# A gated linear recurrence with a two-expert router: another order for the first chunk, and fills moved out of the start

## The chip, the cores and the metric

The kernel runs on one core of a Trainium2 chip. The metric is the device time in microseconds of one execution. A core has a matrix engine (TensorE, PE in the profile; its weight loads are listed apart as PEld), a vector engine (VectorE, DVE), a scalar engine (ScalarE, ACT), a general engine (GpSimd, POOL) and a queue that issues most transfers (SyncE, SP). Each engine works through its own instructions in order and waits at an instruction until what it needs is there.

## What is computed

First a recurrence over 768 steps for 4 batches and 8 heads of width 48. Its rows, 3072 of them with 384 numbers each, are the input of a layer of 8 experts of which each row uses the two with the highest noisy logits:

```python
state = alpha[:, :, t, :, None] * state + einsum('bhd,bhe->bhde', k[:, :, t], v[:, :, t])
y[:, :, t] = einsum('bhd,bhde->bhe', q[:, :, t], state)
...
noisy_logits = x @ w_gate + log1p(exp(x @ w_noise)) * noise
top2 = argpartition(-noisy_logits, 2, axis=1)[:, :2]      # weights: softmax over the two
out[mask] += top2_w[mask, k, None] * (maximum(x[mask] @ w1[e], 0.0) @ w2[e])
```

## The kernel before

The recurrence is worked in 24 chunks (`NT`) of 128 steps, six to a batch. For each chunk there are four loads of 192 KB (alpha, k, q, v). The steps of one chunk are these functions, and the hand-written order of their calls is the order of the instructions on every engine (the block under `manual_schedule`, from L1032 of the profile's numbering):

- `alphas(n)`: TensorE turns the alphas (four transposes, L315), ScalarE copies them from PSUM into `a_all` (L323), VectorE scans them into running products `P_all` (L326), takes a reciprocal (L331) and scans backwards into `over` (L332). There is one `a_all`, one `P_all` and one `over`, so a chunk's scan waits for the readers of the last one's.
- `keys(n)`: four transposes, a copy to `k_P` on ScalarE (L341), a sum on ScalarE that checks the range of the alphas (L344), and on GpSimd the product with `over` (L345).
- `queries(n)`: four transposes, the product with `P_all` on VectorE to `q_P` (L354), and a copy of the last column to `P_end` on GpSimd (L355).
- `scores(n)`: 16 products on TensorE (L365). `masked(n)`: two masked copies on VectorE (L370) into one of two `MT` tiles. `turn_k(n)`: four transposes (L377) and a copy to `k_end` on ScalarE (L379).
- `state(n)`: 16 products (L392), an addition on VectorE (L394), a product on GpSimd (L395).
- `output(n)`: 32 products (L242, L246), a copy on ScalarE (L249). `turn_y(n)`: four products with `to_rows` (L261), which bring the rows and the router's logits, and copies (L264, L267). `put_y(n)` stores the rows.

Iteration n of the main loop holds the later steps of chunk n and the earlier ones of chunks n + 1 and n + 2, loads chunk n + 4, and has the router's steps between. Iteration 0 begins when the steps in front of it are done: all of chunk 0 up to its masked scores, and alphas, keys and queries of chunk 1.

Input tiles rotate over three buffers for each of alpha, k and q. They are 64 columns wide for each head, with 48 of data; the rest is filled once by GpSimd (L281). `transposed` takes its four results from a pool `tp` of two PSUM banks; `output` takes its bank from a pool `y` of one.

Before the loop each engine fills constants: GpSimd the identity, masks, expert numbers and regions (L99 and L100, one column at a time), counters (L105 to L114), the matrix `to_rows` (L171 to L174), the input pads (L281), the states (L300) and the row buffers of the experts, `x_in` and `prev` (L814); VectorE `a_all`, `least` and `MT` (L285 to L296) and a cast of the token numbers from integers (L107), the last before the first scan. `to_rows` is first read in iteration 1, after `place_router` (L188) has put the router's weights into it; `x_in` and `prev` are first written by the gathers from iteration 21 on.

From iteration 23 the tiles of the experts (L871, L883) run beside the last chunks and then alone, up to the end.

Of the kernel before, what the change touches and what calls it, by code (L numbers as in the profile page):

```python
# [9 lines left out]
F32 = mybir.dt.float32  # L10
U32 = mybir.dt.uint32
I32 = mybir.dt.int32
# [6 lines left out]
def kernel(  # L19
# [30 lines left out]
    nc = tc.nc  # L50
    B, H, S, D = q.shape
    N, DM = out.shape
    E, _, F = moe_w1.shape
    C = 128
    DP = 64
# [39 lines left out]
    expert_idv = const.tile([C, EV], F32, name="expert_idv")  # L95
    expert_ids = expert_idv[:, 0:E]
    region = const.tile([C, EV], F32, name="region")
    for e in range(EV):
        nc.gpsimd.memset(expert_idv[:, e:e + 1], float(e))  # L99
        nc.gpsimd.memset(region[:, e:e + 1], float(e * RMAX))  # L100
    before = const.tile([C, C], F32, name="before")
    nc.gpsimd.affine_select(out=before, in_=ones, pattern=[[1, C]], compare_op=ALU.is_gt, fill=0.0, base=0,
                            channel_multiplier=-1)
    token = const.tile([C, NT], I32, name="token")
    nc.gpsimd.iota(token, pattern=[[C, NT]], base=0, channel_multiplier=1)  # L105
    token_f = const.tile([C, NT], F32, name="token_f")
    nc.vector.tensor_copy(out=token_f, in_=token)  # L107
    tile_no = const.tile([C, NTILE], F32, name="tile_no")
    nc.gpsimd.iota(tile_no, pattern=[[1, NTILE]], base=0, channel_multiplier=0, allow_small_or_imprecise_dtypes=True)
    full_at = const.tile([C, RMAX // C], F32, name="full_at")  # L110
# [14 lines left out]
    def clear_table(on):  # L125
        entries.clear()
        nothing = on.tile([C, KO * F], F32, tag="w1", name="nothing")[:, 0:TROWS // C * 4]
        nc.vector.memset(nothing, 0.0)
        nc.vector.memset(nothing.rearrange("p (r w) -> p r w", w=4)[:, :, 0:1], float(NONE))
        cleared = nc.scalar.dma_start(out=table.bitcast(F32).rearrange("(p r) w -> p (r w)", p=C), in_=nothing)  # L130
        entries.append(cleared.ins)
# [21 lines left out]
    def rows(src, n):  # L153
        b, c = divmod(n, NCH)
        return src[b, :, ds(c * C, C), :].rearrange("h p d -> p h d")

    def load_chunk(n, ins):
        for x, src in (("a", alpha), ("k", k), ("q", q)):
            nc.sync.dma_start(out=ins[x][n % NIN][:, :, 0:D], in_=rows(src, n))

    def load_values(n, vp):
        vt = vp.tile([C, H, D], F32, name="vt")
# [5 lines left out]

    to_rows = const.tile([C, NP, 2 * D + 2 * E], F32, name="to_rows")

    nc.gpsimd.memset(to_rows, 0.0)  # L171
    for i in range(2):
        for odd in range(2):
            nc.gpsimd.tensor_copy(  # L174
                out=to_rows.rearrange("p (j o) c -> p j o c", o=2)[:, :, odd, ds(2 * E * odd + D * i, D)],
                in_=ident[:, None, ds(DP * i, D)].to_broadcast([C, NP // 2, D]))

    def load_router(on):
        w_r = on["one"].tile([C, NP, 2, E], F32, name="w_r")
        nc.gpsimd.memset(w_r, 0.0)  # L180
        for w, src in enumerate((moe_w_gate, moe_w_noise)):
            for i, part in enumerate(src.rearrange("(j i d) e -> i d j e", i=2, d=D)):
                nc.sync.dma_start(out=w_r[ds(DP * i, D), :, w, :], in_=part)
        return w_r, load_noise(on)
# [89 lines left out]
    def fast_gla(on):  # L274
# [6 lines left out]
                nc.gpsimd.memset(t[:, :, D:DP], 1.0 if x == "a" else 0.0)  # L281

        CB = C + 1
        a_all = one.tile([C, NP * CB + 1], F32, name="a_all")
        nc.vector.memset(a_all, 0.0)  # L285
        a_s = a_all[:, 0:NP * CB].rearrange("p (j t) -> p j t", t=CB)
        least = one.tile([C, NP, C + 1], F32, name="least")
        nc.vector.memset(least, RANGE)
        nc.vector.memset(least[:, :, 0:1], 1.0)
# [10 lines left out]
            nc.gpsimd.memset(t, 0.0)  # L300
        chunks = {}

        def load(n):
            if n < NT:
                chunks[n] = {}
                load_chunk(n, ins)

        def load_v(n):
            if n < NT:
# [8 lines left out]
        def alphas(n):  # L318
            if n >= NT:
                return  # L320
            c = chunks[n]
            a_t = transposed(ins["a"][n % NIN])
            nc.scalar.copy(a_s[:, :, 1:C + 1], a_t)  # L323
            P_all = one.tile([C, NP * CB + 1], F32, name="P_all")
            P = c["P"] = P_all[:, 0:NP * CB].rearrange("p (j t) -> p j t", t=CB)
            nc.vector.tensor_tensor_scan(P_all[:, 0:NP * CB], a_all[:, 0:NP * CB],  # L326
                                         least.rearrange("p j t -> p (j t)"), 0.0, op0=ALU.mult, op1=ALU.max)


            over = c["over"] = one.tile([C, NP, CB], F32, name="over")  # L330
            nc.vector.reciprocal(out=P_all[:, CB::CB], in_=P_all[:, C::CB])  # L331
            nc.vector.tensor_tensor_scan(over.rearrange("p j t -> p (j t)")[:, :0:-1], a_all[:, :1:-1],  # L332
                                         P_all[:, :1:-1], 0.0, op0=ALU.mult, op1=ALU.max)
# [359 lines left out]
    def put_some(n):  # L693
        for place, entry in to_put[:n]:
            put_entries(place, entry)
        del to_put[:n]
# [111 lines left out]
    def experts(on):  # L808
# [1 line left out]
        NB = 3  # L810
        x_in = [one.tile([C, DM], F32, name=f"x_in{i}") for i in range(NB)]
        prev = [one.tile([C, DM], F32, name=f"prev{i}") for i in range(2)]
        for t in x_in + prev:
            nc.gpsimd.memset(t, 0.0)  # L814
        WHY = "computed from the counts, in range by construction"
        tabs, w1s, xts, os_, wheres = {}, {}, {}, {}, {}
        puts, gets, waiting = [], [], []
# [93 lines left out]
                tc.declare_no_dep(put.ins, earlier, reason="different rows, or one that this tile has read")  # L911
            puts.append(put.ins)

        return load_tab, load_w1, gather_x, turn_x, layer1, layer2, get_first, scale, combine, waiting

    def tile_steps(i, do, units, last=False):
        load_tab, load_w1, gather_x, turn_x, layer1, layer2, get_first, scale, combine, waiting = do

        def first():
            if i + 2 < units[1]:
                gather_x(i + 2, units[0])
            layer1(i, 0)

        def second():
            layer1(i, 1)

        def third():
            if i + 1 < units[1]:  # L930
                turn_x(i + 1)
            if i + 2 < units[1]:
                load_w1(i + 2)
            if i - 1 in waiting:
                waiting.remove(i - 1)
                combine(i - 1)
            if last:
                get_first(i)
            layer2(i, 0)

        def fourth():
            layer2(i, 1)
            if last:
                combine(i)
            else:
                scale(i)
                get_first(i)
                waiting.append(i)

        return [first, second, third, fourth]  # L950

    def pools(es, name):
        on = {"one": pool(name + "one", 1, es), "two": pool(name + "two", 2, es), "three": pool(name + "three", 3, es),
              "tab": pool(name + "tab", 6, es)}
        for x, bufs in (("h", 2), ("o", 1), ("tp", 2), ("sc", 1), ("y", 1)):
            on[x] = pool(name + "ps_" + x, bufs, es, space=PS)
        return on


    def last_tiles(i, do):  # L960
        if i == NTILE:
            return
        number = nc.values_load(tiles_i[0:1, 0:1], min_val=0, max_val=NTILE,
                                skip_runtime_bounds_check_because="a count of tiles")
        with tc.If(number > i):
            do[0](i, NU)
            do[1](i)
            do[2](i, NU)
            do[3](i)
            for step in tile_steps(i, do, (NU, i + 1), True):  # L970
                step()
            last_tiles(i + 1, do)


    def again_by_levels():
        with ExitStack() as es:
            on = pool("g_clear", 1, es)
            clear_table(on)
        with ExitStack() as es:
            general_gla(es)  # L980
        with ExitStack() as es:
            do = experts(pools(es, "g_"))
            for i in range(4):
                do[0](i, NU)
            for i in range(2):
                do[1](i)
                do[2](i, NU)
            do[3](0)
            for i in range(NTILE):
                do[0](i + 4, NU)  # L990
                for step in tile_steps(i, do, (NU, NTILE), i >= NTILE - 1):
                    step()


    with ExitStack() as es:
# [33 lines left out]
        beside = [[] for n in range(TILES_AT)] + [list(range(i, min(i + 2, ALWAYS))) for i in range(0, ALWAYS, 2)]  # L1029
        assert 2 * (NT + 5 - TILES_AT) + 4 <= FULL  # L1030

        with tc.manual_schedule():  # L1032
            load(0)
            load_v(0)
            load(1)
            alphas(0)
            keys(0)
            queries(0)
            load(2)
            scores(0)  # L1040
            masked(0)
            turn_k(0)
            alphas(1)
            keys(1)
            queries(1)
            load_v(1)
            load(3)
            for n, tiles in enumerate(beside):
# [3 lines left out]
                          lambda: more_w2(w2_beside.get(n, 0)), lambda: turn_k(n + 1), lambda: output(n),  # L1052
                          lambda: turn_y(n - 1)]
                chunk = [lambda piece=piece, place=place: (piece(), route(n, place)) for place, piece in enumerate(pieces)]
                last = [lambda: put_some(3)]
                if n > NT:
                    chunk.insert(5, lambda: put_some(3))
# [2 lines left out]
                if n == 1:  # L1060
                    chunk.insert(6, lambda: place_router(held.pop(0)))
                    last.append(lambda: clear_table(on["two"]))
                if n == 2:
                    chunk.insert(1, lambda: turn_noise(held.pop(), on))
                if n == NT + 1:
# [63 lines left out]
```

## Time and profile before

| what | value |
|---|---|
| median of 3 runs | 762.68 us (760.94 to 763.94) |
| the profiled execution: time | 764.23 us |
| its span, first to last instruction | 762.5 us |
| granted TensorE clock, mean | 0.989 |
| TensorE busy | 732.9 us (96%) |
| VectorE, ScalarE, GpSimd busy | 240.9, 184.9, 289.8 us |
| chain that ended last: TensorE's share | 69% |
| its largest lines | L871 28%, L883 26% |

The chain's share by engine says where the program's end comes from: more than half of it is the two layers of the experts. The start is a small part of it, and is read from the timeline.

### The profile page before, as it was taken

To read this page: it belongs to the slowest core of one execution; us is meant where nothing else is said; L and a number is where in the kernel's file an instruction comes from. 1 tells how busy PE (TensorE), PEld (TensorE's weight loads), DVE (VectorE), ACT (ScalarE), POOL (GpSimd) and SP (SyncE) were. 2 spreads that over 40 slices of the span, in tenths; PEclk is the share of its full clock that TensorE was granted. 3 is DMA by queue.
4 is the path that set the end of the run, shared out by engine and by line. 5 is a ranking of instruction groups with operands and counts; after the bars stand their busy time and mean duration, and the time that the engine had idled before them with its cause. 6 is when DMAs were issued, how large, how long until landed. Compare 5 with 4: busy or idle time off the path is not lost.

```text
span 762.5 us, 14806 instructions
## 1 busy us (share of the span) xinstructions
PE 732.9 (96%) x5479; PEld 595.0 (78%) x5479; DVE 240.9 (32%) x778; ACT 184.9 (24%) x385; POOL 289.8 (38%) x409
## 2 busy tenths in 40 slices
PE   5999999997999999999999999999999999999996
PEld 3888877876878778877877887788778877888774
DVE  6777867895011223221111101111111111111111
ACT  3455554452112121111111111111111111111110
POOL 4322474765132544453223332333233323333222
PEclk9999999998899999999999999999999999999999
DMA  9999877878789955654565445544565466556631
GB/s 152 156 150 150 140 124 134 138 162 295 243 214 362 320 179 165 196 206 151 200 225 196 145 176 205 185 164 165 204 213 167 174 209 217 181 170 217 225 131 34
DMA packets 149027, 141.80 MB, mean 186 GB/s; under 512 B 111721, under 2 KB 123607, under 8 KB 148948
## 3 DMA queue, kind: packets, MB, share of 16 engines
q1 hardware_dynamic: 136580, 116.58, 54.3%
q0 software_dynamic: 12224, 23.78, 10.3%
q8 instruction: 47, 0.77, 0.4%
q10 hardware_dynamic: 144, 0.41, 0.2%
q14 instruction: 32, 0.26, 0.1%
HBM read 131.95 MB, written 15.25 MB: 193 GB/s over the span
## 4 chain that ended last, share of the span: by engine, by line
PE 69%; issue 11%; DVE 9%; POOL 4%; DMA 4%; ACT 1%; another core or an unknown queue 0%; POOLq 0%; DVEq 0%; ACTq 0%
PE h_ps L871 28%; PE o_ps L883 26%; PE tp L315 3%; DMA x_in<-x_rows,where 2%; PE h_ps L261 2%; PE y L246 2%; PE x_ps L860 2%; PE y L242 2%; PE sc L365 2%; DMA prev<-out_dram,where 2%; DVE over L332 2%; DVE P_all L326 1%; POOL out_dram L908 1%; DVE MT L370 1%; POOL table L134 1%
## 5 line engine op out<-in xcount | busy, mean ns | idle before, releaser
L871 PEld LDWEIGHTS h_ps<-xt,w 128*128 128x128 f32 x2448 | 284.0, 194 | 14.7 <-DVE again L428 1.6
L871 PE MATMUL h_ps<-xt,w 128*128 128x128 f32 x2448 | 285.0, 277 | 2.1 <-DVE again L428 1.4
L883 PE MATMUL o_ps<-w,h 128*128 x816 | 272.2, 487 | 0.2 <-ACT h L873 0.2
L883 PEld LDWEIGHTS o_ps<-w,h 128*128 128x128 f32 x816 | 151.0, 190 | 95.4 <-issue 0.7
L862 DVE COPY xt<-x_ps 128x384 f32<-128x384 f32 x51 | 28.4, 557 | 390.3 <-PE x_ps L860 308.8
L890 POOL DMA_INDIRECT prev<-out_dram,where x51 | 52.9, 1036 | 234.1 <-DMA out_dram<-prev,where 225.4
L873 ACT ACTIVATE h<-h_ps 128x512 f32<-128x512 f32 x102 | 60.9, 597 | 229.5 <-PE h_ps L871 207.3
L908 POOL DMA_INDIRECT out_dram<-prev,where x51 | 52.3, 1025 | 105.7 <-DVE tab L845 76.4
L899 ACT ACTIVATE o<-o_ps,tab 128x384 f32<-128x384 f32 x49 | 28.4, 580 | 235.3 <-PE o_ps L883 230.7
L851 POOL DMA_INDIRECT x_in<-x_rows,where x51 | 52.7, 1034 | 25.0 <-issue 20.6
L134 POOL DMA_INDIRECT table<-entry,place_u x48 | 49.9, 1039 | 14.0 <-issue 12.8
L315 PE MATMUL tp<-ident,w 128*128 128x128 f32 x288 | 44.5, 291 | 9.0 <-DMA w<-in_alpha_dram 4.2
L345 POOL TENSOR_TENSOR k_P<-k_P,over 128x512 f32<-128x512 f32 x24 | 28.4, 1184 | 58.6 <-DVE over L332 52.2
L904 DVE SCALAR_TENSOR_TENSOR prev<-prev,tab,o 128x384 f32<-128x384 f32 x49 | 30.0, 611 | 59.9 <-DMA prev<-out_dram,where 59.9
L315 PEld LDWEIGHTS tp<-ident,w 128*128 128x128 f32 x288 | 32.3, 146 | 14.7 <-POOL w L281 4.7
L326 DVE TENSOR_TENSOR_SCAN P_all<-a_all,least 128x516 f32<-128x516 f32 x24 | 30.8, 1284 | 16.7 <-ACT a_all L323 8.7
L365 PE MATMUL sc<-q_P,k_P 48*128 48x128 f32 x384 | 30.8, 292 | 3.6 <-POOL k_P L345 3.3
L370 DVE COPY_PREDICATED MT<-upto,sc 128x512 f32<-128x512 uint32 x48 | 32.1, 722 | 2.9 <-PE sc L365 2.9
L365 PEld LDWEIGHTS sc<-q_P,k_P 48*128 48x128 f32 x384 | 25.6, 193 | 8.3 <-issue 4.1
L332 DVE TENSOR_TENSOR_SCAN over<-a_all,P_all 128x515 f32<-128x515 f32 x24 | 30.2, 1259 | 0.8
L860 PE MATMUL x_ps<-ident,x_in 128*128 128x128 f32 x153 | 25.2, 274 | 4.0 <-DMA x_in<-x_rows,where 3.8
L261 PE MATMUL h_ps<-to_rows,yT 128*128 128x112 f32 x192 | 28.5, 293 | 0.5 <-POOL to_rows L188 0.5
(153 smaller groups left out, 483.1 us busy)
## 6 DMA issues: line engine op xcount, KB each, us to landing
w<-in_moe_w_dram SPq DMA_DIRECT2D x51, 1536.0 KB
w<-in_moe_w_dram SPq DMA_DIRECT2D x32, 384.0 KB
w<-in_alpha_dram SPq DMA_DIRECT2D x24, 192.0 KB
w<-in_k_dram SPq DMA_DIRECT2D x24, 192.0 KB
w<-in_q_dram SPq DMA_DIRECT2D x24, 192.0 KB
vt<-in_v_dram SPq DMA_DIRECT2D x24, 192.0 KB
x_rows<-y_sb SPq DMA_DIRECT2D x24, 192.0 KB
x_in<-x_rows,where POOLq DMA_INDIRECT x51
```

The source lines that it names most:

```text
L134: put = nc.gpsimd.indirect_dma_start(out=table, out_offset=bass.IndirectOffsetOnAxis(ap=place, axis=0), in_=entry, in_offset=None, bounds_ ...
L261: nc.tensor.matmul(bank[:, at:at + W], yT[:, j, :], to_rows[:, j, :], start=j == 0, stop=j % 2 == 1, skip_group_check=True)
L315: nc.tensor.transpose(tp[:, j, :], src[:, 2 * j:2 * j + 2, :], ident)
L332: nc.vector.tensor_tensor_scan(over.rearrange("p j t -> p (j t)")[:, :0:-1], a_all[:, :1:-1], P_all[:, :1:-1], 0.0, op0=ALU.mult, op1=ALU.max)
L365: nc.tensor.matmul(c["sc"][i][:, j, :], c["k"][r, j, :], c["q"][r, j, :], start=True, stop=True)
L851: nc.gpsimd.indirect_dma_start(out=x_in[i % NB], out_offset=None, in_=x_rows[0:units * UT, :], in_offset=bass.IndirectOffsetOnAxis(ap=wher ...
L860: nc.tensor.transpose(x_ps[:, a, :], x_in[i % NB][:, ds(a * C, C)], ident)
L871: nc.tensor.matmul(h_ps[:, fo, :], w1[:, a, ds((part * FO // 2 + fo) * C, C)], xt[:, a, :], start=a == 0, stop=a == KO - 1)
L873: nc.scalar.activation(os_[i]["h"][part], h_ps, AF.Relu)
L883: take_w2(i, nc.tensor.matmul(o["ps"], o["h"][part][:, f, :], w2[:, ds(o["e"], 1), fo, :].rearrange("p o d -> p (o d)"), start=fo == 0, st ...
L890: get = nc.gpsimd.indirect_dma_start(out=prev[i % 2].bitcast(U32), out_offset=None, in_=out.bitcast(U32), in_offset=bass.IndirectOffsetOnA ...
L908: put = nc.gpsimd.indirect_dma_start(out=out, out_offset=bass.IndirectOffsetOnAxis(ap=where[:, 0:1], axis=0), in_=rows, in_offset=None, bo ...
```

## The change

It has five parts.

1. Constants. Expert numbers and regions are written by one counter instruction each. The token numbers are counted straight into a float tile; the integer tile and VectorE's cast are gone.
2. Fills. `to_rows` is filled in `load_router`, which is called in iteration 0; `x_in` and `prev` are filled at the end of iteration 2 (`clear_rows`).
3. Two `a_all` tiles take turns, and both are filled at the start.
4. Order. The alphas of chunk 1 are loaded right after chunk 0's alpha, k and q, ahead of v. `alphas(1)` stands in front of `scores(0)`, and `keys(1)` behind it. In iteration 0, `scores(1)` stands ahead of `keys(2)`.
5. Twelve products of `ones` with itself on TensorE whose result is not read: six ahead of `alphas(0)`, one each behind it and behind `keys(0)`, four ahead of `scores(0)`.

```diff
-    for e in range(EV):
-        nc.gpsimd.memset(expert_idv[:, e:e + 1], float(e))
-        nc.gpsimd.memset(region[:, e:e + 1], float(e * RMAX))
+    nc.gpsimd.iota(expert_idv, pattern=[[1, EV]], base=0, channel_multiplier=0, allow_small_or_imprecise_dtypes=True)
+    nc.gpsimd.iota(region, pattern=[[RMAX, EV]], base=0, channel_multiplier=0, allow_small_or_imprecise_dtypes=True)
...
-    token = const.tile([C, NT], I32, name="token")
-    nc.gpsimd.iota(token, pattern=[[C, NT]], base=0, channel_multiplier=1)
     token_f = const.tile([C, NT], F32, name="token_f")
-    nc.vector.tensor_copy(out=token_f, in_=token)
+    nc.gpsimd.iota(token_f, pattern=[[C, NT]], base=0, channel_multiplier=1, allow_small_or_imprecise_dtypes=True)
...
-    nc.gpsimd.memset(to_rows, 0.0)
-    for i in range(2):
...
+    def place_ident():
+        nc.gpsimd.memset(to_rows, 0.0)
+        for i in range(2):
...
     def load_router(on):
         w_r = on["one"].tile([C, NP, 2, E], F32, name="w_r")
         nc.gpsimd.memset(w_r, 0.0)
+        place_ident()
...
-        a_all = one.tile([C, NP * CB + 1], F32, name="a_all")
-        nc.vector.memset(a_all, 0.0)
-        a_s = a_all[:, 0:NP * CB].rearrange("p (j t) -> p j t", t=CB)
+        a_alls = [one.tile([C, NP * CB + 1], F32, name=f"a_all{i}") for i in range(2)]
+        for t in a_alls:
+            nc.vector.memset(t, 0.0)
...
-        for t in x_in + prev:
-            nc.gpsimd.memset(t, 0.0)
+
+        def clear_rows():
+            for t in x_in + prev:
+                nc.gpsimd.memset(t, 0.0)
+
...
+        def warm(times):
+            for _ in range(times):
+                nc.tensor.matmul(on["y"].tile([C, NP, C], F32, tag="y", name="y")[:, 0, :], ones, ones, start=True, stop=True)
+
         with tc.manual_schedule():
             load(0)
+            load(1, "a")
             load_v(0)
-            load(1)
+            load(1, "kq")
+            warm(6)
             alphas(0)
+            warm(1)
             keys(0)
+            warm(1)
             queries(0)
+            alphas(1)
             load(2)
+            warm(4)
             scores(0)
+            keys(1)
             masked(0)
             turn_k(0)
-            alphas(1)
-            keys(1)
             queries(1)
             load_v(1)
             load(3)
...
+                if n == 0:
+                    chunk[2], chunk[3] = chunk[3], chunk[2]
...
+                if n == 2:
+                    last.append(do[-1])
```

More of the change, by code (lines that the diff above doesn't have):

```diff
@@ L155, in rows, with load_chunk @@
         return src[b, :, ds(c * C, C), :].rearrange("h p d -> p h d")
-    def load_chunk(n, ins):
+    def load_chunk(n, ins, parts="akq"):
         for x, src in (("a", alpha), ("k", k), ("q", q)):
-            nc.sync.dma_start(out=ins[x][n % NIN][:, :, 0:D], in_=rows(src, n))
+            if x in parts:
+                nc.sync.dma_start(out=ins[x][n % NIN][:, :, 0:D], in_=rows(src, n))
     def load_values(n, vp):
@@ L169 @@
     to_rows = const.tile([C, NP, 2 * D + 2 * E], F32, name="to_rows")
-    nc.gpsimd.memset(to_rows, 0.0)
-    for i in range(2):
[L173 to L176, printed above, removed]
+    def place_ident():
+        nc.gpsimd.memset(to_rows, 0.0)
+        for i in range(2):
+            for odd in range(2):
+                nc.gpsimd.tensor_copy(
+                    out=to_rows.rearrange("p (j o) c -> p j o c", o=2)[:, :, odd, ds(2 * E * odd + D * i, D)],
+                    in_=ident[:, None, ds(DP * i, D)].to_broadcast([C, NP // 2, D]))
     def load_router(on):
@@ L301, in fast_gla, with load @@
         chunks = {}
-        def load(n):
+        def load(n, parts="akq"):
             if n < NT:
-                chunks[n] = {}
-                load_chunk(n, ins)
+                chunks.setdefault(n, {})
+                load_chunk(n, ins, parts)
         def load_v(n):
@@ L322, in alphas @@
             a_t = transposed(ins["a"][n % NIN])
-            nc.scalar.copy(a_s[:, :, 1:C + 1], a_t)
+            a_all = a_alls[n % 2]
+            nc.scalar.copy(a_all[:, 0:NP * CB].rearrange("p (j t) -> p j t", t=CB)[:, :, 1:C + 1], a_t)
             P_all = one.tile([C, NP * CB + 1], F32, name="P_all")
@@ L912, in combine @@
             puts.append(put.ins)
-        return load_tab, load_w1, gather_x, turn_x, layer1, layer2, get_first, scale, combine, waiting
+        return load_tab, load_w1, gather_x, turn_x, layer1, layer2, get_first, scale, combine, waiting, clear_rows
     def tile_steps(i, do, units, last=False):
-        load_tab, load_w1, gather_x, turn_x, layer1, layer2, get_first, scale, combine, waiting = do
+        load_tab, load_w1, gather_x, turn_x, layer1, layer2, get_first, scale, combine, waiting, clear_rows = do
         def first():
@@ L960, in last_tiles @@
     def last_tiles(i, do):
+        if i == ALWAYS:
+            do[-1]()
         if i == NTILE:
@@ L982, in again_by_levels @@
             do = experts(pools(es, "g_"))
+            do[-1]()
             for i in range(4):
```

## The prediction

> **What bounds the kernel now.** I read the page's slices first, then a table of engine times by stretch, then the first 31 us instruction by instruction, then the DMA queue's own waits.
>
> ```profile
> PE   5999999997999999999999999999999999999996
> ```
>
> From the second slice (19 us each) to the last TensorE is busy. What shortens the program is TensorE work taken out, or TensorE idle time; slice one is half idle. By stretch (length, then busy time and count of PE, PEld, DVE, ACT, POOL, then granted clock, DMA share, GB/s):
>
> ```profile
> 0.00:4.00 4.00, 0.00 (x0) 0.00 (x0) 2.51 (x6) 1.28 (x1) 3.22 (x36) 1.00 0.52 93
> 4.00:8.00 4.00, 3.26 (x12) 2.15 (x12) 4.00 (x3) 1.78 (x4) 4.00 (x18) 1.00 1.48 175
> 8.00:16.00 8.00, 4.90 (x31) 4.22 (x32) 3.71 (x8) 1.52 (x3) 1.38 (x3) 1.00 1.53 166
> 16.00:24.00 8.00, 6.35 (x90) 5.22 (x90) 7.21 (x10) 3.20 (x8) 2.78 (x5) 1.00 1.35 147
> 24.00:32.00 8.00, 7.46 (x107) 6.37 (x104) 6.44 (x11) 4.04 (x10) 2.52 (x7) 1.00 0.89 142
> 32.00:45.00 13.00, 12.98 (x160) 11.06 (x160) 8.76 (x13) 6.37 (x16) 3.10 (x5) 1.00 0.85 166
> ```
>
> The PE column idles 10.0 of the first 32 us and 0.02 of the next 13. So the change is worth what it shifts the point, near 32 us, from which TensorE runs without gaps; later stages move along. Why TensorE idles there, in the timeline (start, us, engine, line):
>
> ```profile
> 4.20 3.46 PE L315 MATMUL tp<-ident,w 128*128 128x128 f32 x12 [4.20 <-DMA w<-in_alpha_dram]
> 4.23 3.88 DVE L107 CAST token_f<-token 128x24 f32<-128x24 int32 x1
> 5.94 2.18 DVE L326 TENSOR_TENSOR_SCAN P_all<-a_all,least 128x516 f32<-128x516 f32 x1
> ...
> 9.78 1.17 POOL L345 TENSOR_TENSOR k_P<-k_P,over 128x512 f32<-128x512 f32 x1 [1.70 <-DVE over L332]
> 10.89 0.19 POOL L355 COPY P_end<-P_all 128x4 f32<-128x4 f32 x1
> 11.00 2.08 PE L365 MATMUL sc<-q_P,k_P 48*128 48x128 f32 x16 [3.34 <-POOL k_P L345]
> ...
> 15.74 1.23 DVE L326 TENSOR_TENSOR_SCAN P_all<-a_all,least 128x516 f32<-128x516 f32 x1 [1.29 <-issue]
> ...
> 19.83 1.16 PE L365 MATMUL sc<-q_P,k_P 48*128 48x128 f32 x16
> ...
> 19.94 1.52 DVE L326 TENSOR_TENSOR_SCAN P_all<-a_all,least 128x516 f32<-128x516 f32 x1 [0.65 <-POOL P_end L355]
> ```
>
> A cast of 24 numbers takes 3.88 us, and chunk 0's scan, normally 1.23, ends with it at 8.12. Chunk 1's scan starts only at 15.74, because its transposes stand behind the scores in TensorE's queue. And the first 16 score products take 2.08 where the next 16 take 1.16.
>
> **The cast.** It runs exactly as long as GpSimd does (4.23 to 8.11; GpSimd is busy to 8.08), so GpSimd's fills may be the reason. The change takes both away, so one answer serves: scan 0 ends at 5.94 + 1.23 = 7.17, 0.95 earlier. The rest of that chain keeps its distances: `over` 0 ends at 8.67, `k_P` 0 at 10.0, `P_end` 0 at 10.13, and the scores can start at 10.05. The second `a_all` fill (0.49 and a gap) puts VectorE's fills at 4.86, 1.1 before the scan: nothing.
>
> **Chunk 1's scan.** It needs `P_end` 0 done (one `P_all` buffer) and its transposes, which now stand ahead of the scores. So it starts at 10.17, not 15.74. VectorE then goes on: `over` 1 11.65 to 12.88, the two masked copies of chunk 0 (1.33) to 14.2, `q_P` 1 (0.67) to 14.86. Before, `q_P` 1 ended at 19.03.
>
> **TensorE beside it.** Scores of chunk 0 10.05 to 11.2 at the later speed (1.16), keys 1 (0.6) to 11.8, turned k (0.5) to 12.3. ScalarE copies `k_P` 1 (0.58), does its sum (0.62 and 0.19), copies `k_end` (0.58): 13.75. State products (0.6) to 14.4, alphas 2 (0.6) to 15.0. So the scores of chunk 1 start at 15.05 instead of 19.83: 4.8 earlier. But before, the keys of chunk 2 already lay in front of them; now they lie behind. From 15.05, scores 1.09, keys 0.59, queries 0.59, turned k 0.44, outputs 1.02 + 1.01, state 0.60, alphas 3 0.54 sum to 5.88: 20.93, against 24.97 (24.43 + 0.54). **4.05 us earlier**, and TensorE is from there on its own bound: the first product with `to_rows` comes at 26.2 instead of 30.21.
>
> **The products nobody reads.** Twelve. Six run in front of the first transposes, from about 1.35 (`ones` is there at 1.27). The trace has no such product; nearest are the slow transposes, 0.27 each in a row (1.09 for four), 0.42 for one alone. Each product writes the bank of the one before and waits for it, so I take 0.42 + 0.07 = 0.49: six end at 4.29, against 4.20 when the alphas come, 0.1 late. Low end 0.27: no delay. High end 0.75 (weights loaded after the wait, 0.2 to 0.3 more): 5.85, 1.65 late. The other six lie in gaps up to 10.05: four transposes of chunk 1 end by 8.3 to 9.1 and four products take 1.3 to 2.0, so at worst they end at 11.0, up to 1.0 late.
>
> What they buy is speed. The granted clock is 1.00 in every row above, yet four transposes take 1.09 at 4.20 and 0.66 at 15.71, some 4.3 us after the scores began. [...] they do speed up. [...] the scores may stay slow: 0.92 more, slow transposes 0.5 each for two groups, together 1.45 later at the scores of chunk 1, a gain of 2.6. By the row the gain is 4.05. I take the row: [...] products and transposes together fill 1.35 to 9 us with short gaps.
>
> **Fills moved to GpSimd's later iterations.** `to_rows` (0.46 + 0.88) now stands in iteration 0 behind the multiplication of the state (ends 15.75), and ends at 17.25; the next thing queued there, `k_P` 2, is due at 18.7. The five row buffers (five times 0.38) stand at the end of iteration 2 between `P_end` 4 and the multiplication of the state. In the old run those end at 38.49 and start at 40.58: 2.1 us for 1.9, and the outputs that read that state come 2.0 later still. Nothing; without that cover 1.9. [...] the scan at 19.94 took 1.52 beside 0.43 us of GpSimd's multiplication, 0.29 more. Filling `to_rows` lies beside chunk 2's scan for 1.35, by that rate up to 0.9 more. [...] `q_P` 2 and `k_P` 2 are ready at 19.2 and 19.9 where TensorE comes to their scores at 21.6, and chunk 3's scan waits for its alphas until 21.7 (VectorE free at 20.85). So 0, at most 0.1.
>
> **Loads.** SP issues the same ones, with alphas 1 as the fourth instead of the fifth. From 8 to 22 us the DMA moves 163 GB/s, so I estimate that load n (0.197 MB) has landed when n + 1 are moved: alphas 1 at 7.5, keys 1 9.9, queries 1 11.1, alphas 2 12.3, keys 2 13.5, alphas 3 17. They are wanted at 8, 11.2, 12.3, 14.4, 16.1, 20.4: all in time, by 0.5 at the least. The router's weights are issued behind them, from 20.49 to 24.32, and their last bytes move at 25.3; they can come 0.8 earlier at most, and are now wanted at 25.9. Cost 0 to 0.5, taken 0. In the steady stage loads wait for buffers, not the reverse (the queue's waits: us, times, longest):
>
> ```profile
> SPq L163 <- PE y L246: 48.6, 18, 5.5
> ```
>
> **Sum.** 4.05 from a run of 764.23 us (span 762.5): span 758.45, 760.2 with what lies around it. That run was 1.55 over the median of 762.68, so in terms of the median **758.6**.
>
> **Rivals.**
> - *The start stays slow*: products cost 0.75 each, or the scores run at the slow rate. For it: the self-waits[...]. Against: 0.42 for a lone slow transpose. Gain 1.5 to 2.8, some 760.3. Chance 0.15.
> - *The loads set the pace*, so an earlier start only waits at iteration 3. For it: DMA share 1.5 up to 22 us, five transfers of 0.197 MB per 6.85 us chunk are 144 GB/s of some 165. Against: the share drops to 0.08 at 23.5 to 24, and the line just shown. Then only SP's earlier issue counts, 0.4: 762.3. Chance 0.1.
> - *Slower*: the unread products hold TensorE's in-order queue in front of the first transposes, and everything follows those. With price p each the transposes are 6p - 2.85 late; the gain is used up at p = 1.15. At 1.3, 763.6. The lone 0.42 speaks against it. Chance 0.05.
> - *The full shift, or somewhat more* (fast clock already at the first transposes saves 0.5 more): gain 3.3 to 5.2, 757.5 to 759.4. Chance 0.7.
>
> The range reaches from 756.7 to 761.0: all of the last, most of the first. About 0.5% (3.8 us) is what a measurement here can tell from no change; the forecast of 0.53% lies just beyond it. From the cases: 0.60 faster, 0.34 within, 0.06 slower.
>
> **What would show it.** In the new profile: no cast, first scan 1.23 long and ending near 7.2; second scan near 10.2; first scores in about 1.16, near 10; scores of chunk 1 near 15; first `to_rows` product near 26.2; the stretch 32 to 45 without PE gaps. First transposes later than 4.4 would mean that the products cost more than I took; gaps on waits for DMA after 20 us, that the loads pace it; a late `to_rows` product, that the router's weights do.

## The result and the profile after

The changed kernel takes 758.23 us (median of 4 runs, 757.41 to 759.08), the kernel before 762.58 (4 runs, 760.94 to 763.94). The ratio is 0.9944, with a 95% interval of 0.9921 to 0.9967: 4.3 us less. The profiled execution took 759.08 us, with a span of 757.4.

TensorE's row of the page, again in slices of a fortieth of the span, has a first slice of 8 tenths instead of 5. The changed kernel by stretch (length, then busy time and count of PE, PEld, DVE, ACT, POOL, then granted clock, DMA share, GB/s):

```profile
0.00:4.00 4.00, 2.50 (x7) 1.62 (x7) 2.46 (x7) 1.28 (x1) 3.22 (x25) 1.00 0.48 95
4.00:8.00 4.00, 3.88 (x15) 3.30 (x16) 0.96 (x2) 0.59 (x1) 0.63 (x3) 1.00 1.03 201
8.00:16.00 8.00, 6.87 (x65) 5.45 (x63) 6.94 (x10) 3.44 (x8) 2.33 (x3) 1.00 1.06 211
16.00:24.00 8.00, 7.68 (x106) 6.49 (x102) 6.13 (x11) 3.91 (x8) 5.37 (x12) 1.00 0.65 120
24.00:32.00 8.00, 7.48 (x90) 6.17 (x87) 5.50 (x9) 3.60 (x10) 2.12 (x5) 1.00 0.81 163
32.00:45.00 13.00, 13.00 (x172) 11.21 (x172) 9.48 (x14) 6.51 (x18) 4.93 (x10) 1.00 0.60 144
```

TensorE now idles 3.6 of the first 32 us instead of 10.0, but much of the difference is filled with the unread products. The second thing to see is at the end of the rows. From 8 to 16 us the DMA moved 211 GB/s at a share of 1.06; before, 166 at 1.53. Nothing in the prediction said so.

The start, in the timeline of the changed kernel:

```profile
1.33 5.06 PE L1042 MATMUL y<-ones 128*128 128x128 f32 x12 [1.33 <-POOL ones L91]
2.18 0.50 PEld L1042 LDWEIGHTS y<-ones 128*128 128x128 f32 x2 [0.35 <-PE y L1042]
...
6.18 1.06 PE L315 MATMUL tp<-ident,w 128*128 128x128 f32 x4
...
7.90 1.23 DVE L327 TENSOR_TENSOR_SCAN P_all<-a_all,least 128x516 f32<-128x516 f32 x1 [3.04 <-ACT a_all L324]
...
12.01 1.16 PE L366 MATMUL sc<-q_P,k_P 48*128 48x128 f32 x16 [0.29 <-POOL k_P L346]
12.12 1.23 DVE L327 TENSOR_TENSOR_SCAN P_all<-a_all,least 128x516 f32<-128x516 f32 x1 [0.92 <-POOL P_end L356]
...
16.80 1.16 PE L366 MATMUL sc<-q_P,k_P 48*128 48x128 f32 x16
...
28.09 1.15 PE L261 MATMUL h_ps<-to_rows,yT 128*128 128x112 f32 x8 [0.50 <-POOL to_rows L188]
```

The six products in front (twelve records, two each) fill TensorE from 1.33 to 6.4: the weights of each wait until the one before is done (0.35 us on L1042), and one follows the next every 0.85 us. The first transposes start at 6.18, 1.98 later than before, and everything behind them with them. The first product with `to_rows` comes at 28.09: 2.1 earlier than the old 30.21, not 4.05.

Where the rest of the gain lies is told by the start of each chunk's first scan, in the two profiled executions (us; difference in the last column):

| mark | before | after | gained so far |
|---|---|---|---|
| chunk 0's scan | 5.94 | 7.90 | -1.96 |
| chunk 1 | 15.74 | 12.12 | 3.62 |
| chunk 3 | 25.84 | 23.71 | 2.13 |
| chunk 9 | 67.57 | 65.39 | 2.18 |
| chunk 12 | 88.12 | 85.95 | 2.17 |
| chunk 17 | 127.11 | 120.04 | 7.07 |
| chunk 23 | 173.45 | 166.36 | 7.09 |
| first tile of the experts (its copy of x) | 189.34 | 182.96 | 6.38 |
| tile 50 | 739.47 | 734.38 | 5.09 |

The start brought 2.2, the chunks 12 to 17 another 4.9, and 2.0 were lost again up to tile 50 of the experts. Between 80 and 140 us TensorE was busy 57.17 us before and 59.42 after. Where it stood in chunks 12 to 17 of the old run is seen in its timeline:

```profile
101.08 3.73 SPq L159 DMA_DIRECT2D w<-in_q_dram  x1
...
118.40 0.58 ACT L323 COPY a_all<-tp 128x512 f32<-128x512 f32 x1 [2.72 <-remote]
...
119.04 0.66 PE L315 MATMUL tp<-ident,w 128*128 128x128 f32 x4 [1.31 <-issue]
```

A load that is mostly issued in about 1 us took 3.73. Later ScalarE stood 2.72 us in front of the alphas of a chunk, for a release that the profile puts down to none of the core's engines, and TensorE's next transposes came right behind that copy, after 1.31 us of idle time. That the load is the cause is not shown: in the changed kernel a load at 97.60 took 2.93 us to issue, and TensorE's idle times in these chunks were 0.4 us at most. So two questions were open: what each part of the start is worth, and why the loads are faster.

### The profile page after: what moved, and what is told of

Read it like the earlier page. It is cut to its first block, busy times and chain, and to the rows that moved or that the text cites. A ratio compares the mean times of both kernels' runs of the same rounds, so it can differ in the third digit from the quotient of the medians.

```text
span 757.4 us, 14848 instructions
## 1 busy us (share of the span) xinstructions
PE 734.3 (97%) x5503; PEld 597.0 (79%) x5503; DVE 240.5 (32%) x778; ACT 185.0 (24%) x385; POOL 294.1 (39%) x393
## 4 chain that ended last, share of the span: by engine, by line
PE 66%; issue 11%; DVE 7%; DMA 7%; POOL 5%; ACT 1%; SPq 0%; POOLq 0%; DVEq 0%; ACTq 0%
PE h_ps L875 27%; PE o_ps L887 25%; DMA prev<-out_dram,where 4%; PE tp L315 3%; DMA x_in<-x_rows,where 3%; PE h_ps L261 2%; PE y L242 2%; PE y L246 2%; PE x_ps L864 2%; POOL out_dram L912 2%; PE sc L366 2%; DVE over L333 1%; DVE P_all L327 1%; PE o_ps L393 1%; DVE MT L371 1%
```

## The experiments

The kernels below ran in three groups of four, each on one chip with its own runs of the kernel before: 762.45 us in the first group, 768.1 and 768.0 in the others. So times are compared as ratios within a group, and the start by the scan of chunk 3 or 9, which comes from a trace.

**Both kernels once more** (no edit).

> The kernel before once more, for a second trace. Theory S (the gain of 4.9 us between the scans of chunks 12 and 17 is a property of the changed order): this trace again waits there, chunk 17's scan near 127 and chunk 12's near 88. Theory R (waits for loads there come and go from run to run): the distance from chunk 12's scan to chunk 17's, 39.0 us in the first trace of before and 34.1 in that of after, lies anywhere between. Both expect the entry into the gapless stage unchanged: chunk 9's scan at 67.6, within 0.3. Time: 762.6, within 1.5.

> The changed kernel once more, for a second trace. Both theories expect chunk 9's scan at 65.4, within 0.3 (2.15 earlier than before). Theory S expects 34 us from chunk 12's scan to chunk 17's, as in its first trace; theory R allows 34 to 39. Time: 758.2, within 1.5.

Measured: chunk 9's scan at 67.60 and 65.64, so the start repeats. Ratios 0.9992 (0.9970 to 1.0013) and 0.9944 (0.9926 to 0.9962). From chunk 12's scan to chunk 23's 84.35 and 80.42 us; the first two traces had 85.33 and 80.41. That spoke for S, a property of the changed kernel, and on this chip it held: the two variants that follow took 80.41 as well. On the chips of the other groups it did not: there the same stretch took 85.0 to 90.5 us in variants of either kernel.

**Without the unread products.**

```diff
-            for _ in range(times):
+            for _ in range(0):
```

> The changed kernel without the twelve unread products. Theory P (six products at 0.85 each in front of the first transposes put the whole start 1.98 late, and their clock is worth less): first transposes at 4.2 instead of 6.18, and chunk 9's scan 0.5 to 2.0 earlier than in after, 63.4 to 64.9. Theory C (the clock is worth more than the wait): the first scores take 2.08 and the transposes behind them 1.06 a group, and chunk 9's scan is at 65.4 or later. In time P expects 756.3 to 757.8, C 758.2 or more.

TensorE's timeline of this variant:

```profile
3.96 4.18 PE L315 MATMUL tp<-ident,w 128*128 128x128 f32 x16 [3.96 <-POOL w L281]
9.80 2.08 PE L366 MATMUL sc<-q_P,k_P 48*128 48x128 f32 x16 [1.66 <-POOL k_P L346]
```

Both theories were partly right. The transposes start 2.2 earlier, and the scores are slow again (2.08 instead of 1.16). Net, chunk 9's scan is at 65.02, 0.4 to 0.6 earlier than with the products: on P's side, and just outside its 63.4 to 64.9. As written, the products cost the start a little more than they bring. Time 757.58, ratio 0.9936 (0.9912 to 0.9960), against 0.9944: not told apart.

**The products of one call in one tile**, so that they do not wait for each other.

```diff
-            for _ in range(times):
-                nc.tensor.matmul(on["y"].tile([C, NP, C], F32, tag="y", name="y")[:, 0, :], ones, ones, start=True, stop=True)
+            y = on["y"].tile([C, NP, C], F32, tag="y", name="y")
+            for i in range(times):
+                nc.tensor.matmul(y[:, i % NP, :], ones, ones, start=True, stop=True)
```

> The changed kernel with the unread products of one call written to slices of one tile, so that none of a call waits for the one before it. Theory P: each costs 0.25 to 0.3 instead of 0.85, six end near 3.0, the first transposes start at 4.2 and, if the clock is up by the first scores (1.16), chunk 9's scan is at 63.3 to 63.6, 2 us earlier than in after, time 756.3. Theory C': the shorter stretch of products no longer brings the clock up in time, the first scores take 2.08, chunk 9's scan at 64.3 to 65.

The same lines of this variant:

```profile
1.33 2.93 PE L1043 MATMUL y<-ones 128*128 128x128 f32 x12 [1.33 <-POOL ones L91]
4.05 1.06 PE L315 MATMUL tp<-ident,w 128*128 128x128 f32 x4
...
5.33 0.72 PE L315 MATMUL tp<-ident,w 128*128 128x128 f32 x4
...
9.86 1.16 PE L366 MATMUL sc<-q_P,k_P 48*128 48x128 f32 x16 [1.59 <-POOL k_P L346]
```

The twelve records are through by 4.26 and leave the transposes where the alphas let them start, and the scores run at the fast rate (1.16). The speed comes sooner, too: the four transposes at 5.33 take 0.72, while in the changed kernel those at 7.46 still took 1.06. Chunk 1's scores start at 14.65, chunk 9's scan at 63.24: 4.33 earlier than before, a little ahead of P's 63.3. P's price was wrong, though: it had the six end near 3.0, at 0.25 to 0.3 each, and they cost 2.93 / 6 = 0.49. At the start the products are worth 65.02 - 63.24 = 1.78 us if they wait for nothing. Time 754.75 (6 runs), against 757.54 for the changed kernel in this group; ratio 0.9916 (0.9882 to 0.9949).

**Only the cast taken out of the kernel before.**

```diff
-    token = const.tile([C, NT], I32, name="token")
-    nc.gpsimd.iota(token, pattern=[[C, NT]], base=0, channel_multiplier=1)
+    const.tile([C, NT], F32, name="gap")
     token_f = const.tile([C, NT], F32, name="token_f")
-    nc.vector.tensor_copy(out=token_f, in_=token)
+    nc.gpsimd.iota(token_f, pattern=[[C, NT]], base=0, channel_multiplier=1, allow_small_or_imprecise_dtypes=True)
```

> The kernel before with only the cast taken out: token numbers are counted into the float tile, and the place of the integer tile stays empty, so that no tile moves. The cast's own theory: scan 0 is 1.23 long, and chunk 9's scan comes 0.95 earlier, 66.65. Rival (GpSimd's fills, which still run to 8.08, hold VectorE, not the cast): scan 0 still ends near 8.1 and chunk 9's scan stays at 67.6. Middle stage as in before, 84.4 to 85.3 us; time 762.6 or 761.6.

One row of its stretches and one of its timeline:

```profile
4.00:8.00 4.00, 3.26 (x12) 2.15 (x12) 2.14 (x4) 1.77 (x4) 4.00 (x18) 1.00 1.44 176
```

```profile
6.11 1.23 DVE L325 TENSOR_TENSOR_SCAN P_all<-a_all,least 128x516 f32<-128x516 f32 x1 [1.79 <-ACT a_all L322]
```

GpSimd (fifth pair) is still busy for all of the 4 us, and yet the scan takes 1.23. So the fills do not hold a scan; the cast did (2.18 with it). Why the cast itself took 3.88 us is not shown: no run kept it and took the fills away. Chunk 9's scan is at 66.76, 0.84 earlier. Ratio 0.9990 (0.9971 to 1.0010): in time, nothing that can be told.

**Where the input buffers lie.** The dropped integer tile has 24 numbers, 96 bytes per partition, and stood ahead of the large tile `w2`, whose end serves as the input buffers at the start. In the built program `w2` begins at byte 21856 before and at 21760 after. First, a shift by 32 in each kernel:

```diff
+    const.tile([C, 8], F32, name="gap1")
     w2 = const.tile([C, E, FO, DM], F32, name="w2")
+    const.tile([C, 8], F32, name="gap2")
```

> The kernel before with 32 unused bytes per partition ahead of the tile that holds the input buffers (and 32 behind it, so that all later tiles keep their place within 64 bytes). The buffers start at byte 21888, a multiple of 64, instead of 21856. Theory L (the place of the buffers sets the rate of the loads, and with it the waits between chunks 12 and 23; the change moved them to a multiple of 64 when it dropped the integer tile): DMA share from 8 to 16 us falls from 1.53 to about 1.05, the rate there rises from 166 to about 200 GB/s, chunk 12's scan to chunk 23's takes 80.4 us instead of 84.4 to 85.3; chunk 9's scan stays at 67.6; time 4 us less, about 758.3. Theory O (the changed order, loads or fills do it): share 1.53, 84 to 85 us, time unchanged.

> The changed kernel with the same 32 bytes ahead of the input buffers, which puts them at 32 behind a multiple of 64, as before. Theory L: DMA share 1.5 from 8 to 16 us at 163 GB/s, 84 to 85 us from chunk 12's scan to chunk 23's, time about 762. Theory O: 1.05, 80.4 us, 757.8. By both, chunk 9's scan stays near 65.5, or comes later where the slow loads are late at the start.

The rows for 8 to 16 us, first of the shifted kernel before, then of the shifted changed one:

```profile
8.00:16.00 8.00, 4.96 (x29) 4.33 (x30) 3.71 (x8) 1.19 (x3) 1.42 (x3) 1.00 1.52 166
```

```profile
8.00:16.00 8.00, 7.25 (x49) 5.93 (x47) 6.94 (x10) 3.41 (x8) 2.28 (x3) 1.00 1.03 204
```

Theory L fell: the share did not follow multiples of 64 (1.52 at one, 1.03 off one). Ratios 1.0004 (0.9979 to 1.0029) and 0.9952 (0.9931 to 0.9973). One mark missed both theories: chunk 9's scan of the shifted changed kernel came at 67.24 instead of 65.5. In that execution the granted clock was 0.96 from 24 to 32 us and 0.90 from 32 to 45. But the four places fit another rule. The buffers hold rows of 192 bytes, one every 256. Behind a multiple of 256 they start at 96 (before), 128 (before, shifted), 0 (after) and 32 (after, shifted): the first two lie across the next multiple (shares 1.53 and 1.52), the last two do not (1.06 and 1.03). The next pair put each kernel's rows where the other's had been, with gaps of 40 and 24 numbers around `w2` in the kernel before, 24 and 40 in the changed one:

```diff
+    const.tile([C, 40], F32, name="gap1")
     w2 = const.tile([C, E, FO, DM], F32, name="w2")
+    const.tile([C, 24], F32, name="gap2")
```

> The kernel before with 160 unused bytes ahead of the tile with the input buffers and 96 behind, so that each 192-byte row of alpha, k and q starts at a multiple of 256 instead of 96 behind one; all later tiles move by 256. Theory W (rows that lie across a multiple of 256 are slow to write; before and the first shifted variant have them at 96 and 128 behind it, both across; the changed kernel and its shifted variant at 0 and 32, neither across): DMA share from 8 to 16 us falls from 1.53 to 1.0, rate from 166 to 200 GB/s, share from 60 to 80 us from 0.89 to 0.67. Theory O (what the change does to the order or to GpSimd's fills decides the rate): 1.53 and 0.89. Chunk 9's scan 67.6 by both. If the rate is also what the waits between chunks 12 and 23 hang on, their distance falls toward that of the changed kernel (80.4 or 85.0 on the two chips seen) and time by 2 to 4 us; if they hang on something else, time is unchanged.

> The changed kernel with 96 unused bytes ahead of the input buffers, so that they lie at the same address as before, across multiples of 256. Theory W: share 1.5 and 163 GB/s from 8 to 16 us, 0.89 from 60 to 80 us; keys and queries of chunks 1 and 2 may come late, chunk 9's scan at 65.6 to 67. Theory O: 1.0 and 0.67, chunk 9's scan at 65.6. Time, if the rate counts for the middle stage: 2 to 4 us above the changed kernel, no gain over before but the 2.1 of the start; if not: as the changed kernel, 0.9945 of before.

From 60 to 80 us in the two unmoved kernels, before and after:

```profile
60.00:80.00 20.00, 20.00 (x261) 17.09 (x260) 16.49 (x43) 11.98 (x30) 5.40 (x9) 1.00 0.89 144
60.00:80.00 20.00, 20.00 (x261) 17.07 (x260) 16.50 (x45) 11.91 (x30) 5.47 (x9) 1.00 0.67 144
```

The kernel before with its rows at multiples of 256, then the changed one with rows across them:

```profile
8.00:16.00 8.00, 4.99 (x30) 4.36 (x31) 3.71 (x8) 1.21 (x3) 1.39 (x3) 1.00 1.03 204
60.00:80.00 20.00, 20.00 (x261) 17.08 (x260) 16.49 (x43) 11.99 (x30) 5.41 (x9) 1.00 0.66 143
```

```profile
8.00:16.00 8.00, 7.16 (x57) 5.87 (x55) 6.95 (x10) 3.44 (x8) 2.33 (x3) 1.00 1.52 167
60.00:80.00 20.00, 20.00 (x262) 17.09 (x259) 16.54 (x45) 11.72 (x29) 5.47 (x9) 1.00 0.78 140
```

The DMA columns follow the place of the rows, whatever the kernel: theory W, though from 60 to 80 us the changed kernel came to 0.78 only, not 0.89. In time, the kernel before gains by the move alone: 0.9970 (0.9950 to 0.9989), 2.3 us. The changed kernel with rows across takes 0.9993 (0.9975 to 1.0011) of before: no gain can be told, though chunk 9's scan came at 65.56, 2.0 earlier than in the unchanged start. So by the first of the two about half of the 4.3 us came with the 96 bytes, which nobody moved for that.

How much it is in the changed kernel is not settled. With rows not across, that kernel did not run on this chip. The nearest that did (the fills back at the start, below) takes 765.31 against 767.80 with rows across, and its start alone is 2.3 earlier, so little is left there for the place. The moved tile also takes the second layer's weights later; no run moves the input buffers alone. Nor do the traces show where the time is won. From chunk 12's scan to chunk 23's, one trace each, in us:

| traces | rows not across | rows across |
|---|---|---|
| the first two, and the first group | 80.41, 80.42, 80.41, 80.41 | 85.33, 84.35 |
| second group | 84.98, 86.92 | 88.51, 86.72 |
| third group | 87.64, 85.43, 90.52 | 88.42 |

In the first row the stretch goes with the place in every trace; in the other two it does not clearly.

**The old order of calls in the variant with one tile**: `alphas(1)` and `keys(1)` behind `turn_k(0)`, no exchange in iteration 0.

```diff
-            alphas(1)
             load(2)
             warm(4)
             scores(0)
-            keys(1)
             masked(0)
             turn_k(0)
+            alphas(1)
+            keys(1)
             queries(1)
...
-                if n == 0:
-                    chunk[2], chunk[3] = chunk[3], chunk[2]
```

> The faster variant (unread products in one tile) with the old order of the calls: scores of chunk 0 ahead of the alphas of chunk 1, and in iteration 0 keys of chunk 2 ahead of the scores of chunk 1. It measures the reordering by itself with the clock up. Worked out from that variant's durations: chunk 1's scan at 12.7 instead of 9.97, scores of chunk 1 2.1 later but with one group of transposes already done, so chunk 9's scan 1.5 later than 63.24: 64.7. Rival (the clock was all, the order hides behind TensorE's queue): 63.3.

Chunk 1's scan starts at 12.81, as expected. Chunk 3's is 1.36 later than in the variant (22.92 to 21.56), chunk 9's 2.7 later (65.97). The last is not the order alone: in this run the granted clock was 1.00 up to 24 us, 0.88 from 24 to 32 and 0.94 from 32 to 45. So the order is worth about 1.4 us at the start, close to the 1.5 worked out, and the rival is wrong. The ratio, 0.9949 (0.9927 to 0.9972), does not resolve it: the next variant, on the same chip and with the new order, has 0.9958.

**The fills back at the start**, in the variant with one tile: `place_ident()` called where it is defined, the row buffers filled in `experts`.

```diff
         nc.gpsimd.memset(w_r, 0.0)
-        place_ident()
...
-        def clear_rows():
-            for t in x_in + prev:
-                nc.gpsimd.memset(t, 0.0)
+        for t in x_in + prev:
+            nc.gpsimd.memset(t, 0.0)
```

> The faster variant with the fills of the row buffers and of the matrix for rows back at the start. Prediction's claim (the place of the fills is worth nothing): GpSimd is done by about 7.7, before it is wanted at 8.6, chunk 9's scan at 63.24 within 0.1. Rival (fills on GpSimd slow VectorE's first scan, or the input pads behind them come late): scan 0 longer than 1.23 or chunk 9's scan 0.3 to 1 later.

Chunk 9's scan at 63.26, the first scan 1.23 long: at the start the place of the fills is worth nothing. For the whole time that is not shown. The ratio is 0.9958 (0.9941 to 0.9975); the same kernel with late fills had 0.9916 on the first chip and, with a small shift, 0.9877 on the second (next experiment), whose interval does not overlap. Chip or fills: no run has both places on one chip.

**v and the weights at multiples of 64**: 32 bytes behind `w2` in the variant with one tile.

```diff
     w2 = const.tile([C, E, FO, DM], F32, name="w2")
+    const.tile([C, 8], F32, name="gap2")
```

> The faster variant (unread products in one tile) with 32 unused bytes behind the large tile, so that the tiles of v, of the first layer's weights and of the stored rows start at multiples of 64 too. If the place counts for these as well, the DMA share falls below 1.05 from 8 to 16 us, and waits for rows in the expert stage shorten: under 754. If it counts for the 192-byte rows of alpha, k and q alone: 754.75 within 1, stages as in that variant (chunk 9's scan at 63.2, 80.4 us).

Share 1.04 from 8 to 16 us, chunk 9's scan at 63.26: no difference in either. The stretch from chunk 12's scan took 86.92 us, not 80.4. The ratio is 0.9877 (0.9840 to 0.9914), which overlaps that of the variant itself on another chip (0.9882 to 0.9949). In time the question it was made for stays undecided. That products in one tile beat both kernels is seen on two chips, in 6 and 7 runs (760.29 here, against 765.46 for the shifted changed kernel); on the third, the two kernels that have them, with the old order or the early fills, do not show it.

## Why the prediction came out

The time was forecast at 758.6 and measured at 758.23. That the number came out is luck: one term of the sum was too small by 1.9 us, and a gain of about the same size, which the prediction put at nothing, made up for it.

- **The price of the unread products failed.** I took 0.49 each, 0.07 of it my estimate for the wait; they cost 0.85, with a wait of 0.35, above my high end of 0.75. The six end their hold on TensorE at 6.18 instead of 4.29. The prediction named the sign of it, first transposes later than 4.4. The start gained 2.15, which was the first rival's range (1.5 to 2.8, given a chance of 0.15).
- **The rest of the start's sum held.** The forecast 4.05, less the 1.98 by which the transposes came late, is 2.07; measured at the marks is 2.1 to 2.2. And with one tile, where the six do cost 0.49 each, chunk 1's scan is at 9.97 (forecast 10.17), its scores at 14.65 (15.05), chunk 9's scan 4.33 earlier (4.05). The cast alone is 0.84 (0.95).
- **The clock**, as the prediction and the expectations call TensorE's faster rate: the first scores took 1.16, as taken. The granted clock does not show this rate: it reads 1.00 from 8 to 16 us in both kernels, with first scores of 2.08 before and 1.16 after. I was right that transposes run faster later on, too (with one tile 1.06 for the four at 4.05, 0.72 for those at 5.33). But I took it that transposes help to bring the fast scores, and alone they did not: in the run without products, 4.18 us of them in a row left the scores at 2.08, and with products among them the scores took 1.16; the idle time in front of the scores was about the same (1.66 us, and 1.59 with one tile). What part transposes have in the faster rate, and what brings it on, one run without products can't say. The terms named for slow scores, 0.92 and twice 0.5, sum to 1.92, not to 1.45.
- **The fills** cost nothing at the start. That of `to_rows` ended at 20.37, not at 17.25, since its copies were slow (last section); `k_P` 2, behind it, waited until 20.31 for `over` anyhow. The row buffers stand in their gap in the changed kernel's GpSimd timeline, with 0.35 to spare:

```profile
36.12 0.19 POOL L356 COPY P_end<-P_all 128x4 f32<-128x4 f32 x1
36.24 1.13 POOL L817 MEMSET x_in<- 128x384 f32 x3
37.32 0.78 POOL L817 MEMSET prev<- 128x384 f32 x2
38.45 0.51 POOL L396 TENSOR_TENSOR S<-S,P_end 128x192 f32<-128x192 f32 x1 [0.35 <-DVE S L395]
```

- **The loads failed.** (From 8 to 22 us they moved 167 GB/s, not 163; nothing hangs on that.) "SP issues the same ones" was true, and I looked no further than their order. The dropped tile moved where they land, and the term put at nothing is worth 2.3 us (0.8 to 3.8) in the kernel before. In the changed one 0.9993 and 0.9944 would make it 3.7, but they come from different chips, and on the third chip alone little is left for it.
- **The rival of the loads** did not come true: the first `to_rows` product waited for GpSimd (the line at 28.09), and from 32 to 45 us TensorE was busy for all of the 13. Whether later chunks wait for loads is not shown. Between 85 and 180 us the profiles of both kernels put nearly all of TensorE's idle time down to other engines or to none (2.9 us of "issue" in the kernel before), and 0.2 at most to a load.

What stays open: where the faster rate pays, and why the stretch from chunk 12 to 23 goes with it in the first group and not clearly in the others; why 2.0 us were lost again in the expert stage; and why the start's 2.0 us leave only 0.5 in time where the rows lie across. The interval of the last, 1.4 us to either side, reaches 1.9.

## What to carry to other kernels

Filler products that are to bring TensorE up to speed should write where none waits for the one before (here 0.49 us each instead of 0.85, and first scores of 1.16 us with them, 2.08 without); price them by such a pair in a trace, not by a lone product. When a tile comes or goes, look where all tiles behind it land, and at the DMA share and GB/s of a stage whose loads "did not change" (here 96 bytes went with 1.06 and 211 instead of 1.53 and 166). A right total is no proof of its terms: compare the marks of the stages.

## What the runs showed of the hardware

- Loads of 192-byte rows were slow where the rows cross a multiple of 256 in SBUF: from 8 to 16 us a share of 1.52 or 1.53 at 166 or 167 GB/s in three kernels with rows at 96 or 128 behind one, 1.03 to 1.06 at 204 to 211 GB/s in three with rows at 0 or 32. The DMA tables of 8 to 16 us (packets, MB, share of 16 engines), first the kernel before, then the changed one:

```profile
q1 hardware_dynamic: 7037, 1.33, 152.6%
```

```profile
q1 hardware_dynamic: 8932, 1.69, 106.3%
```

That is 27.8 and 15.2 ns for a packet (share times 16 times 8 us over the count), over all loads of these 8 us, v's too. The packet time grew 1.8 times. Within a pair of places the runs show no difference (shares 1.06 and 1.03 at 0 and 32, 1.53 and 1.52 at 96 and 128). Why a row across costs more is not shown.
- A chained product (each waits for the last) cost 0.85 us at the slow rate (the six in front) and 0.54 at the fast one (the four from 9.70); unchained, the six took 2.93. The granted clock of the changed kernel reads 1.00 from 0 to 16 us, over both rates, so this change is not seen in that column.
- GpSimd's four copies into `to_rows` were slower in iteration 0, beside VectorE's scans of chunk 2, than at the start. First in the kernel before, then in the changed kernel:

```profile
3.72 0.88 POOL L174 COPY to_rows<-ident 128x96 f32<-128x96 f32 x4
```

```profile
18.12 2.25 POOL L173 COPY to_rows<-ident 128x96 f32<-128x96 f32 x4
19.01 1.30 DVE L333 TENSOR_TENSOR_SCAN over<-a_all,P_all 128x515 f32<-128x515 f32 x1
```

The four copies took 2.25 us instead of 0.88, the backward scan beside them 1.30 instead of 1.23. With the fills back at the start that scan took 1.23; in two variants with the copies in iteration 0 (rows across, old order) it took 1.30. What makes the copies slow is not shown.
